# Fixed places for the first expert's weight preparation, another order at the head, and the products with v on GpSimd

## The chip, the cores and the metric

The kernel runs on one core of a Trainium2 chip. A core has a matrix engine, TensorE (PE in the profile, with its weight loads listed apart as PEld), and four more: VectorE (DVE), ScalarE (ACT), GpSimd (POOL) and SyncE (SP, which only issues DMAs here). Each engine runs its own queue strictly in order, and the queues meet through semaphores. The metric is the time of one execution on the device, in microseconds (us); a comparison is made with the median of several executions.

## The reference

Two layers follow each other. The first is a linear attention with a decaying state (B = 4 batches, H = 8 heads, S = 768 tokens, D = 48), the second a mixture of experts on its output (N = 3072 tokens of 384 features, E = 8 experts, F = 1024 hidden features, two experts a token):

```python
for t in range(S):
    cur = np.einsum('bhd,bhe->bhde', u[None] * k_t, v_t)
    y[:, :, t] = np.einsum('bhd,bhde->bhe', r_t, state + cur)
    state = w[None, :, :, None] * state + np.einsum('bhd,bhe->bhde', k_t, v_t)
x = y.transpose(0, 2, 1, 3).reshape(N, 384)

noisy = x @ w_gate + np.log1p(np.exp(x @ w_noise)) * noise
top2, top2_w = the two largest of each row, and their softmax
for e in range(E):
    for k in range(2):
        mask = top2[:, k] == e
        h = np.maximum(x[mask] @ w1[e], 0.0)
        out[mask] += top2_w[mask, k, None] * (h @ w2[e])
```

The term with `u` is the token's own: for each head it is the scalar c = sum over d of r, u and k, times the row v. This product `c * v` is called `cv` below.

## The kernel before

**Attention.** The tokens are cut into 24 tiles of 128 tokens of one batch (chunk c of 6, batch b of 4; tile i = 4c + b). For a tile, `kd` is k times powers of the decay (`prep_k`, GpSimd, two half products), `kT` and `rT` are transposes of k and r (PE `pt`, then ACT and DVE, `trans`), `pa` the scores (`scores`), `am` the scores behind the causal mask (`mask`, DVE), `py` the output from scores and state (`yout`), `pwarm` the update of the state (`kvup`), which `zup` folds into `z` and `zb`. For the token's own term GpSimd forms `rku` in four half products (`uterm_a`), DVE sums it to `c`, and `cv` is formed from `c` and `vt` in `uterm_b` (L321 to L327): in one DVE product up to tile 8, in eight ACT products, one a head, from tile 9 on. `x` = `py` + `cv` is made on DVE (`xout`) and stored to DRAM by SP; its transposes (`ptx`, `xT`) give the router's logits (`pl`, `lg`).

The program order is written out by hand: each engine's queue has the order in which the code emits. One pass of the tile loop works on several tiles at once: loads of tile i+3, `trans(i+1)`, `xtrans(i-1)`, `zup(i-1)`, `uterm_b(i+1)`, `prep_k(i+2)`, `uterm_a(i+2)`, weight steps, routing steps, `yout(i)`, `xout(i)`, `logits(i-1)`, routing steps, `scores(i+1)`, `mask(i+1)`, `kvup(i)`, routing steps.

**Routing.** After each group of 8 tiles (`GROUPS`) a long list of small DVE operations on the logits (`route`: softplus, the two largest, counts per expert) and a few matmuls into `RT` follows. It is a generator; `rstep` advances it by a given amount of credit at each point of the program where it is called, and after a step that waits for PE it skips `gap[0]` calls. `r_om` is the 0/1 matrix of chosen experts; its matmuls (L626 to L629) count the tokens ahead in each expert's list. `drop` builds the lists: from the comparisons `r_oa` and `r_ob` matmuls into `RT` (L523) put each token's number into its slot. The list of expert 0 has 7 columns of 128 slots, the lists of the other seven experts (`rest`, `drop_all`) have 49.

**Weights.** Each matmul of the experts is split for precision: a weight is a high part, `w..h` (ACT copy, L279), and the rest, `w..l` (DVE subtraction, L281), both from a staging buffer `stg` of three that one SP DMA fills. An expert has 7 units of this kind (three of w1, four of w2). A unit is a generator with stops: load, `NLAG[0]` stops, high part, stop, low part. `wstep()` moves up to three units in flight by one stop each; in the tile loop it is called twice a tile up to tile 10 and once from then on.

**Experts.** `seq` lists (expert, chunk of its token slots); expert 0 has chunks of 2, 2 and 3 tiles of slots, the last tile with 64 rows. `xgather` (GpSimd, indirect DMA) fetches rows of x, `xT` transposes them (PE `ptm`) into `xh` and `xl`, `p1` computes the hidden layer (`ph`, then `hb` on ACT and DVE, `ht` for the 64-row tile), `p2` the second matrix (`pym`, `ot`), `emit_out` scales, adds and scatters. While expert 0 runs, `rstep` and `rest_step` spread the rest of the routing over `p1` and `p2`, and `wstep` prepares expert 1's weights.

## Time and profile before

| | |
|---|---|
| median of three runs | 660.09 us (659.82 to 660.27) |
| the profiled execution | 659.12 us |
| its span, first to last instruction | 657.4 us |
| PE busy | 626.2 us (95%) |
| DVE, ACT, POOL busy | 349.4, 262.7, 262.9 us (53, 40, 40%) |
| mean granted PE clock | 0.987 |
| share of the chain that ended last: PE, DVE, ACT | 83, 11, 2% |

The span is cut into stretches below; "idle before" of an instruction is the time in which its engine had nothing to do ahead of it, with the instruction whose end released it. PE is busy nearly throughout, so what matters is where it is not, and where its clock is below full.

### The profile page before, as it was taken

What the parts mean: (1) busy time and instruction counts of PE and PEld (TensorE: products, weight loads), DVE (VectorE), ACT (ScalarE), POOL (GpSimd) and SP (SyncE); (2) the same over time, 40 slices, a digit from 0 to 9 for tenths busy, and PEclk for the clock granted to TensorE, in tenths of its full rate; (3) what the DMA queues carried; (4) which work ended last, traced back from release to release, by engine and by line L of the source; (5) the groups of instructions that cost most, each with busy time, mean ns of one, the idle gap of its engine ahead of it and who ended that gap; (6) DMA issues with size and microseconds to landing.
All of it is one profiled execution on the core that took longest, in us unless ns stands there. A gap on an engine that the chain in (4) does not pass through costs nothing.

```text
span 657.4 us, 11894 instructions
## 1 busy us (share of the span) xinstructions
PE 626.2 (95%) x4436; PEld 595.4 (91%) x4437; DVE 349.4 (53%) x883; ACT 262.7 (40%) x737; POOL 262.9 (40%) x389
## 2 busy tenths in 40 slices
PE   7999889999997889999999999999999999999993
PEld 4998789998897879999999999999999999999993
DVE  8786778797479935253452525345252534523230
ACT  1566656775323424243251524325152433523210
POOL 8775526453101247313631641363174136315211
PEclk9999979999999999999999999999999999999997
DMA  8997667773204535242533434253343425302101
GB/s 128 233 227 175 133 142 164 162 174 101 81 1 153 184 118 167 90 133 74 182 107 104 152 98 134 71 183 100 111 153 96 132 72 181 95 26 86 37 2 37
DMA packets 111444, 78.87 MB, mean 120 GB/s; under 512 B 86721, under 2 KB 101441, under 8 KB 111378
## 3 DMA queue, kind: packets, MB, share of 16 engines
q1 hardware_dynamic: 101442, 49.19, 30.2%
q0 software_dynamic: 9936, 28.83, 14.0%
q8 instruction: 37, 0.61, 0.4%
q14 instruction: 29, 0.24, 0.1%
HBM read 59.03 MB, written 19.76 MB: 120 GB/s over the span
## 4 chain that ended last, share of the span: by engine, by line
PE 83%; DVE 11%; ACT 2%; issue 2%; DMA 0%; POOL 0%; POOLq 0%; DVEq 0%; SPq 0%
PE ph L857 31%; PE pym L891 30%; PE py L396 5%; PE pa L346 3%; PE ptm L832 3%; DVE am L354 2%; PE pl L426 2%; PE py L388 2%; PE pym L884 2%; PE pt L334 2%; PE pym L882 2%; PE pwarm L364 1%; DVE RT L454 1%; PE ptx L414 1%; ACT cv L327 1%
## 5 line engine op out<-in xcount | busy, mean ns | idle before, releaser
L891 PE MATMUL pym<-w1h,hb 128*128 128x384 f32 x768 | 204.2, 339 | 0.0
L912 POOL DMA_INDIRECT out_dram<-ot,TK x56 | 57.6, 1029 | 219.9 <-DVE ot L908 200.6
L857 PE MATMUL ph<-xh,w0h 128*128 128x384 f32 (+3 forms) x408 | 142.3, 349 | 1.7 <-ACT xh L833 1.7
L891 PEld LDWEIGHTS pym<-w1h,hb 128*128 128x128 f32 x768 | 139.4, 188 | 1.1 <-issue 0.3
L857 PE MATMUL ph<-xl,w0h 128*128 128x384 f32 (+3 forms) x408 | 139.6, 342 | 0.5 <-DVE xl L834 0.2
L857 PE MATMUL ph<-xh,w0l 128*128 128x384 f32 (+3 forms) x408 | 139.4, 342 | 0.0
L861 DVE SCALAR_TENSOR_TENSOR hb<-ph,hb 128x384 fp32r<-128x384 f32 (+1 forms) x136 | 72.4, 532 | 113.9 <-ACT ht L859 68.4
L891 PE MATMUL pym<-w1l,hb 128*128 128x384 f32 x384 | 129.3, 337 | 0.0
L859 ACT ACTIVATE hb<-ph 128x384 fp32r<-128x384 f32 (+1 forms) x136 | 64.3, 473 | 120.0 <-PE ph L857 112.4
L897 ACT ACTIVATE ot<-pym 128x384 f32<-128x384 f32 x45 | 22.1, 492 | 160.4 <-PE pym L891 155.8
L805 POOL DMA_INDIRECT xg<-xd,GR x56 | 54.0, 964 | 80.1 <-DVE f L687 35.1
L857 PEld LDWEIGHTS ph<-xh,w0h 128*128 128x128 f32 x408 | 77.1, 189 | 5.1 <-ACT xh L833 2.4
L857 PEld LDWEIGHTS ph<-xl,w0h 128*128 128x128 f32 x408 | 77.1, 189 | 3.7 <-DVE xl L834 1.2
L857 PEld LDWEIGHTS ph<-xh,w0l 128*128 128x128 f32 x408 | 77.2, 189 | 2.6
L891 PEld LDWEIGHTS pym<-w1l,hb 128*128 128x128 f32 x384 | 72.2, 188 | 0.1
L834 DVE TENSOR_TENSOR xl<-ptm,xh 128x384 fp32r<-128x384 f32 (+1 forms) x56 | 28.9, 524 | 74.3 <-ACT xh L833 63.3
L814 POOL DMA_INDIRECT pv<-out_dram,GA x49 | 55.6, 1134 | 25.9 <-issue 14.9
L396 PE MATMUL py<-vt,am 128*128 128x96 f32 x384 | 60.8, 284 | 2.9 <-DVE am L354 2.0
L396 PEld LDWEIGHTS py<-vt,am 128*128 128x128 f32 x384 | 52.0, 197 | 5.1 <-DVE am L354 4.8
L307 POOL TENSOR_TENSOR kd<-kt,tabk 128x192 f32<-128x192 f32 x46 | 27.4, 617 | 57.8 <-PE pwarm L364 50.6
L281 DVE TENSOR_TENSOR w1l<-stg,w1h 128x768 fp32r<-128x768 f32 x32 | 30.8, 961 | 10.2 <-ACT w1h L279 10.2
L354 DVE TENSOR_TENSOR am<-pa,mneg 128x512 int32<-128x512 int32 x48 | 30.7, 680 | 8.8 <-PE pa L346 6.9
(205 smaller groups left out, 865.8 us busy)
## 6 DMA issues: line engine op xcount, KB each, us to landing
stg<-in_moe_w_dram SPq DMA_DIRECT2D x24, 512.0 KB, 4.2
stg<-in_moe_w_dram SPq DMA_DIRECT2D x32, 384.0 KB, 3.3
rd<-in_r_dram SPq DMA_DIRECT2D x24, 192.0 KB, 4.5
vt<-in_v_dram SPq DMA_DIRECT2D x24, 192.0 KB, 4.1
xd<-x SPq DMA_DIRECT2D x24, 192.0 KB, 2.0
out_dram<-zrow SPq DMA_DIRECT2D x16, 288.0 KB, 3.7
kt<-in_k_dram SPq DMA_DIRECT2D x23, 192.0 KB, 3.3
xg<-xd,GR POOLq DMA_INDIRECT x56
```

The costliest lines, as they stand in the source:

```text
L281: nc.vector.tensor_sub(lo, tv, hi.bitcast(F32))
L307: (eng or nc.gpsimd).tensor_mul(kd[i % 3][:, h, :D], kt[i][:, h], tabk[:, h, :D])
L354: nc.vector.tensor_tensor(am[:, s].bitcast(I32), pa[s].bitcast(I32), mneg.to_broadcast([128, NP, 128]), op=ALU.bitwise_and)
L396: nc.tensor.matmul(o2, AM[i][:, s, p, :], vt[i][:, h, None, :].to_broadcast([128, 2, D]), start=not c and h == 0, stop=h == H - 1, skip_gr ...
L805: nc.gpsimd.indirect_dma_start(out=xg[:n], out_offset=None, in_=xd[:GROUPS[GEARLY - 1][1] * 128] if early_ else xd, in_offset=bass.Indirec ...
L814: nc.gpsimd.indirect_dma_start(out=pv[:n], out_offset=None, in_=out, in_offset=bass.IndirectOffsetOnAxis(ap=GA[:n, e * NJ + t:e * NJ + t + ...
L834: nc.vector.tensor_sub(xl[:, :, o:o + n], pt[:, :, :n], xh[:, :, o:o + n].bitcast(F32))
L857: nc.tensor.matmul(ph[:, :w_], a[:, d, fs], x[:, d, :w_], start=(j == 0), stop=(j == len(q) - 1))
L859: nc.scalar.activation(h_[:, f, 0, :], ph[:, a:b], AF.Relu)
L861: nc.vector.scalar_tensor_tensor(h_[:, f, 1, :], ph[:, a:b], 0.0, h_[:, f, 0, :].bitcast(F32), op0=ALU.max, op1=ALU.subtract)
L891: nc.tensor.matmul(py, hb[:, f, a, hs], x[:, f, :], start=(j == 0), stop=(j == len(q) - 1))
L912: st = nc.gpsimd.indirect_dma_start(out=out, out_offset=bass.IndirectOffsetOnAxis(ap=TK[:n, q:q + 1], axis=0), in_=ot[:n], in_offset=None, ...
```

## The change

Four edits come together. **Weights of expert 0:** the three tables `W_LD`, `W_HI` and `W_LO` say at which tile each of the seven units is loaded, gets its high part and its low part; the calls of `wstep` in the tile loop are gone. Units 0 to 4 are finished by tile 8, the high parts of units 5 and 6 come in tiles 21 and 22, the low parts in tile 22 and behind the loop. The load and the low part stand at the end of a tile's pass, the high part where `wstep` stood. **The head:** the loads come in the order k0, r0, k1, v0, r1, u, v1; one copy of the decay's powers goes from DVE to ACT, `w128` comes later, `prep_k(1)` ahead of `uterm_a(0)`, and `prep_k(0)` with `uterm_b(0)` behind `trans(1)`. **The products `cv`** of tiles 9 to 23 are two half products on GpSimd (128 x 192 each) in place of eight on ACT. **Between attention and expert 1:** `p2(0,0)` steps the routing every 8 matmuls with a third of the credit; `gap[0]` stays 2 where it was set to 1; the credit in `p2(0,1)` is 1.2 for 1.0 and in `p1(0,2)` 1.1 for 0.75; in `p1(0,2)` expert 1's weights and next transposes get no step, in `p1(1,0)` the weights get two a step; and the transposes of expert 1's first tiles may start in `p2(0,2)` once the lists are done.

```diff
@@ -37,6 +37,10 @@
 XT_AT = 4
 LREP = 6
 NOT = 4
+
+W_LD = {1: (0,), 2: (1, 2), 4: (3,), 5: (4,), 6: (5,), 7: (6,)}
+W_HI = {4: (0,), 5: (1,), 6: (2,), 7: (3,), 8: (4,), 21: (5,), 22: (6,)}
+W_LO = {4: (0,), 5: (1,), 6: (2,), 7: (3,), 8: (4,), 22: (5,)}
 
 
 @with_exitstack
@@ -123,10 +127,12 @@
             dst[i] = t
 
     load(0, (0, 2))
+    load(1, (0, 1))
+    load(0, (2, 3))
+    load(1, (1, 2))
     ub = const.tile([128, H, D], F32, name="ub")
     nc.sync.dma_start(ub, bass.AP(tensor=u.tensor, offset=u.offset, ap=[[0, 128], [1, H * D]]))
-    load(0, (2, 3))
-    load(1)
+    load(1, (2, 3))
     load(2)
     wg = const.tile([128, ND, 2 * E], F32, name="wg")
     nc.sync.dma_start(wg[:, :, :E], w_gate.rearrange("(c p) e -> p c e", p=128))
@@ -174,9 +180,8 @@
     nc.vector.reciprocal(pwk[:, :, 64:80], tmpw[:, :, 0:16])
     nc.vector.tensor_mul(pwk[:, :, 80:96], pwk[:, :, 64:80], pwk[:, :, 79:80].to_broadcast([128, NP, 16]))
     nc.vector.tensor_mul(pwk[:, :, 96:128], pwk[:, :, 64:96], pwk[:, :, 95:96].to_broadcast([128, NP, 32]))
-    nc.vector.tensor_copy(pwr[:, :, 0:64], pwk[:, :, 127:63:-1])
+    nc.scalar.activation(pwr[:, :, 0:64], pwk[:, :, 127:63:-1], AF.Copy)
     w128 = const.tile([128, NP, 1], F32, name="w128")
-    nc.vector.tensor_mul(w128, tmpw[:, :, 63:64], tmpw[:, :, 63:64])
 
     kT, rT = {}, {}
     for src, store, pw, nm in ((kd[0], kT, pwk, "kT"), (rd[0], rT, pwr, "rT")):
@@ -193,6 +198,7 @@
     warm(WARM1)
     nc.scalar.activation(tabk.rearrange("p h d -> p (h d)"), ptab.rearrange("p a b -> p (a b)"), AF.Copy)
 
+    nc.vector.tensor_mul(w128, tmpw[:, :, 63:64], tmpw[:, :, 63:64])
     acc = const.tile([128, E], BF16, name="acc")
     spacer = const.tile([1, 1], F32, name="spacer")
     Z = [att.tile([128, NP, D], F32, name=f"z{b}", bufs=1) for b in range(B)]
@@ -258,7 +264,7 @@
 
 
     W = {}
-    NLAG = [4]
+    NLAG = [1]
 
     def w_split(e):
         W[e] = {}
@@ -323,8 +329,8 @@
         if i <= GROUPS[0][1]:
             nc.vector.tensor_mul(cv, vt[i], c8.to_broadcast([128, H, D]))
         else:
-            for h in range(H):
-                nc.scalar.activation(cv[:, h, :], vt[i][:, h, :], AF.Copy, scale=c8[:, h, :])
+            for h in (slice(0, H // 2), slice(H // 2, H)):
+                nc.gpsimd.tensor_mul(cv[:, h], vt[i][:, h], c8[:, h].to_broadcast([128, H // 2, D]))
         CV[i] = cv
 
     def trans(i):
@@ -921,16 +927,14 @@
     hold = []
 
 
-    wq.extend(w_split(0))
+    wun = w_split(0)
     consts_a()
+    prep_k(1)
     uterm_a(0)
-    prep_k(1)
     uterm_a(1)
     consts_b()
     scores(0)
     mask(0)
-    prep_k(0, nc.vector)
-    uterm_b(0)
     warm(WARM3)
     route_q = []
 
@@ -980,6 +984,9 @@
                               zrow[:96, None, :].to_broadcast([96, 2, DM]))
         if i + 1 < NT:
             trans(i + 1)
+        if i == 0:
+            prep_k(0, nc.vector)
+            uterm_b(0)
         if i:
             xtrans(i - 1)
             zup(i - 1)
@@ -992,8 +999,8 @@
         if i + 2 < NT:
             prep_k(i + 2)
             uterm_a(i + 2)
-        for _ in range(0 if i < 2 else 2 if i < 11 else 1):
-            wstep()
+        for p in W_HI.get(i, ()):
+            next(wun[p])
         rstep(STEPS_A)
         if i == 0:
             flag = consts_c()
@@ -1014,20 +1021,20 @@
             mask(i + 1)
         kvup(i)
         rstep(STEPS_KV)
+        for p in W_LO.get(i, ()) + W_LD.get(i, ()):
+            next(wun[p])
     xtrans(NT - 1)
     next(p1a)
     logits(NT - 1)
     route_when_done(NT - 1)
-    while wq or wrun:
-        wstep()
+    next(wun[6])
     NLAG[0] = 3
     for j, _ in enumerate(p1a):
         if j == XT_AT_0:
             for _ in xT(0, 1):
                 pass
         rstep(STEPS_P1)
-    for t in p2(0, 0):
-        rstep(STEPS_P2)
+    for t in p2(0, 0, lambda: rstep(STEPS_P2 / 3)):
         hold.append((0, t))
     def routes_done():
         rows(EARLY // 128, NJ)
@@ -1065,8 +1072,7 @@
             xgather(1, 0)
             tokens(NJ, E * NJ)
 
-    gap[0] = 1
-    for t in p2(0, 1, lambda: rest_step(1.0)):
+    for t in p2(0, 1, lambda: rest_step(1.2)):
         if t == 3:
             for _ in xT(0, 2):
                 pass
@@ -1086,15 +1092,18 @@
             while hold:
                 emit_out(*hold.pop(0))
             if s == 2:
-                rest_step(STEPS_P1)
-            elif XT_AT <= j < XT_AT + 2:
+                rest_step(1.1)
+                continue
+            if XT_AT <= j < XT_AT + 2:
                 next(xt, None)
             wstep()
+            if s == 3:
+                wstep()
         if s > 2 and s + 2 < len(seq):
             xgather(*seq[s + 2])
 
         for t in p2(e, ci, (lambda: rest_step(1.0)) if s == 2 else None):
-            if s > 2:
+            if s > 2 or listed[0] and t > chunks(e)[ci][0]:
                 next(xt, None)
             wstep()
             hold.append((e, t))
```

How the queues stand is seen in three places. The first is DVE in the pass of tile 10, where `r_s`, `r_sn` and `RT` are the routing list of the first group. Before:

```order
L339 TENSOR_TENSOR rT<-pt,pwr 128x512
L375 TENSOR_TENSOR zt<-pwarm,z_185 128x192
L321 TENSOR_REDUCE c_1201<-rku 128x8
L281 TENSOR_TENSOR w1l_720<-stg,w1h_719 128x768
L583 TENSOR_TENSOR r_s_1139<-RT,r_d 128x64
L584 SCALAR_TENSOR_TENSOR r_sn<-RT,nz 128x64
L586 TENSOR_SCALAR RT<-r_s_1139 128x64
L589 SCALAR_TENSOR_TENSOR RT<-RT,r_s_1139 128x64 x4
L404 TENSOR_TENSOR x<-py,cv 128x384
```

And with the change:

```order
L345 TENSOR_TENSOR rT<-pt,pwr 128x512
L381 TENSOR_TENSOR zt<-pwarm,z_185 128x192
L327 TENSOR_REDUCE c_1187<-rku 128x8
L589 TENSOR_TENSOR r_s_1125<-RT,r_d 128x64
L590 SCALAR_TENSOR_TENSOR r_sn<-RT,nz 128x64
L592 TENSOR_SCALAR RT<-r_s_1125 128x64
L595 SCALAR_TENSOR_TENSOR RT<-RT,r_s_1125 128x64 x4
L410 TENSOR_TENSOR x<-py,cv 128x384
```

The low part `w1l` no longer stands between `c` and the routing list, nor anywhere ahead of `x` in this pass; line numbers are 6 higher. The second place is GpSimd's queue in the same part of the program, where `kd` of a tile is followed by `rku` of it. Before:

```order
L307 TENSOR_TENSOR kd_83<-kt,tabk 128x4x48 x2
L314 TENSOR_TENSOR rku<-rd_87,kt 128x192 x2
L316 TENSOR_TENSOR rku<-rku,ub 128x192 x2
L307 TENSOR_TENSOR kd_84<-kt,tabk 128x4x48 x2
L314 TENSOR_TENSOR rku<-rd_88,kt 128x192 x2
L316 TENSOR_TENSOR rku<-rku,ub 128x192 x2
```

And with the change:

```order
L313 TENSOR_TENSOR kd_83<-kt,tabk 128x4x48 x2
L320 TENSOR_TENSOR rku<-rd_87,kt 128x192 x2
L322 TENSOR_TENSOR rku<-rku,ub 128x192 x2
L333 TENSOR_TENSOR cv<-vt,c_980 128x192 x2
L313 TENSOR_TENSOR kd_84<-kt,tabk 128x4x48 x2
L320 TENSOR_TENSOR rku<-rd_88,kt 128x192 x2
L322 TENSOR_TENSOR rku<-rku,ub 128x192 x2
L333 TENSOR_TENSOR cv<-vt,c_1080 128x192 x2
L313 TENSOR_TENSOR kd_85<-kt,tabk 128x4x48 x2
```

One pair `cv` a tile stands ahead of `kd` and `rku` of the tile behind it, from tile 9 on. The third place is PE between expert 0's first and second chunk: `pym` is the end of `p2(0,0)`, `ph` belongs to `p1(0,1)`. Before:

```order
L857 MATMUL ph<-xh,w0h_455 128x256
L857 MATMUL ph<-xl,w0h_455 128x256
L857 MATMUL ph<-xh,w0l_456 128x256
L626 LDWEIGHTS ltri
L626 MATMUL RT<-r_om,ltri 128x64
L628 LDWEIGHTS ones_b
L628 MATMUL RT<-r_om,ones_b 128x56
L628 LDWEIGHTS ones_b
L628 MATMUL RT<-r_om,ones_b 128x48
```

And with the change:

```order
L897 MATMUL pym<-w1l_673,hb 128x384
L897 MATMUL pym<-w1h_672,hb 128x384
L632 LDWEIGHTS ltri
L632 MATMUL RT<-r_om,ltri 128x64
L634 LDWEIGHTS ones_b
L634 MATMUL RT<-r_om,ones_b 128x56
L634 LDWEIGHTS ones_b
L634 MATMUL RT<-r_om,ones_b 128x48
```

The count matmuls of the last group (`RT<-r_om`) stood behind two of the eight hidden blocks of `p1(0,1)` and now stand ahead of the first, directly behind `pym`. In the third chunk, `p1(0,2)`, the three `w1l` that stood between the steps `r_ob` of the lists on DVE are gone; they now stand in `p1(1,0)`.

## The prediction

> **What bounds the kernel now.** I read the page's busy time and slices first, then stretches of the span, then the timeline of each engine around the stretches where TensorE is short of work.
>
> ```profile
> PE 626.2 (95%) x4436; PEld 595.4 (91%) x4437; DVE 349.4 (53%) x883; ACT 262.7 (40%) x737; POOL 262.9 (40%) x389
> ```
> ```profile
> PEclk9999979999999999999999999999999999999997
> ```
> ```profile
> 20.00:40.00 20.00, 20.00 (x248) 18.94 (x249) 15.62 (x27) 11.24 (x31) 14.05 (x25) 1.00 1.09 238
> 240.00:260.00 20.00, 17.97 (x96) 17.23 (x95) 10.98 (x18) 9.41 (x22) 13.71 (x15) 0.91 0.45 128
> 300.00:400.00 100.00, 100.00 (x567) 96.27 (x566) 43.21 (x83) 38.61 (x96) 42.88 (x52) 1.00 0.38 116
> ```
> Behind the start and length of a stretch stand the busy times of PE, PEld, DVE, ACT and POOL, then PE's granted clock. From 300 to 400 us PE is never idle, and the change edits nothing there. So the gain or loss lies in the 31.2 us (657.4 less 626.2) in which PE idles and in the two stretches at a lower clock, around 80 to 100 and 240 to 260 us. The next view cuts the attention phase at the starts of its logits matmuls (`pl`), one row a tile (i = 8 to 12):
>
> ```profile
> 55.32:61.58 6.26, 6.26 (x76) 5.99 (x74) 5.07 (x8) 4.47 (x12) 3.93 (x6) 1.00 0.58 113
> 61.58:69.34 7.76, 6.71 (x75) 6.07 (x74) 4.91 (x11) 3.80 (x12) 4.22 (x7) 1.00 0.77 190
> 69.34:77.12 7.78, 6.86 (x75) 6.13 (x75) 6.83 (x23) 5.72 (x22) 3.36 (x6) 1.00 0.85 172
> 77.12:90.09 12.97, 9.66 (x75) 8.85 (x74) 7.36 (x37) 7.37 (x26) 4.12 (x6) 0.74 0.47 106
> 90.09:96.38 6.29, 6.29 (x74) 6.02 (x74) 4.61 (x19) 3.67 (x12) 3.35 (x6) 1.00 0.78 167
> ```
> An undisturbed tile takes 6.26 us, all of it PE. Three in a row take 1.50, 1.52 and 6.71 us more.
>
> **The change part by part: weights of expert 0 and `cv`.** In tile 8 and tile 10 the same thing happens:
>
> ```profile
> 77.84 1.92 ACT L327 ACTIVATE cv<-vt,c 128x48 f32<-128x48 f32 x8
> 79.66 0.83 ACT L279 ACTIVATE w1h<-stg 128x768 fp32r<-128x768 f32 x1
> ```
> ```profile
> 62.34 1.16 PE L346 MATMUL pa<-rT,kT 64*128 64x128 f32 x16
> ```
> ```profile
> 64.25 1.06 DVE L281 TENSOR_TENSOR w1l<-stg,w1h 128x768 fp32r<-128x768 f32 x1 [2.98 <-ACT w1h L279]
> 65.24 0.55 DVE L404 TENSOR_TENSOR x<-py,cv 128x384 f32<-128x384 f32 x1
> ```
> ```profile
> 73.53 1.22 DVE L354 TENSOR_TENSOR am<-pa,mneg 128x512 int32<-128x512 int32 x2
> ```
> ```profile
> 80.53 0.96 DVE L281 TENSOR_TENSOR w1l<-stg,w1h 128x768 fp32r<-128x768 f32 x1 [4.05 <-ACT w1h L279]
> ```
> ```profile
> 83.68 0.66 PE L414 MATMUL ptx<-ident,x 128*128 128x128 f32 x2 [3.12 <-DVE RT L591]
> ```
> `w1l` heads the DVE queue and waits for `w1h`, which stands on ACT behind eight `cv` products (1.92 us). Behind `w1l` stand the routing list and `x`, and PE's transposes of `x` wait 3.12 us. The clock then falls to half (0.74 over 12.97 us is 6.7 us at half): 3.12 of waiting and some 3.4 of slow matmuls make the 6.71. In the change no weight stands in tiles 9 to 20 and no `cv` on ACT from tile 9, so tile 10 loses its chain: -6.7. In tile 8 `w1l` comes behind `am`, not ahead of `x`: -1.5. But tile 9 now carries that `w1l`. In the trace's timeline DVE runs without rest from the end of `x` (65.71) to `am` at 73.53, 7.8 us; with the 1.06 of `w1l` it is 8.9, and the tile is bound by DVE. That stretch can begin when the scores are ready, 63.5 (62.34 plus 1.16), so 2.2 us sooner; less 1.06, `am` comes 1.1 us sooner, not the 1.5 that tile 8 gains: +0.35. Bounds for the three tiles together: -8.2 (the +0.35 hidden) and -2.6 (tile 10 keeps 5.2, rival C).
>
> **`cv` on GpSimd.** The trace has no such product there. Its nearest rows are the queue's own:
>
> ```profile
> 92.45 1.16 POOL L307 TENSOR_TENSOR kd<-kt,tabk 128x192 f32<-128x192 f32 x2 [8.87 <-PE pwarm L364]
> 93.56 1.15 POOL L314 TENSOR_TENSOR rku<-rd,kt 128x192 f32<-128x192 f32 x2
> 94.67 1.14 POOL L316 TENSOR_TENSOR rku<-rku,ub 128x192 f32<-128x192 f32 x2
> 98.95 0.60 POOL L307 TENSOR_TENSOR kd<-kt,tabk 128x192 f32<-128x192 f32 x1 [3.14 <-PE pwarm L364]
> ```
> ```profile
> 94.47 0.54 DVE L321 TENSOR_REDUCE c<-rku 128x8 f32<-128x384 f32 x1
> ```
> ```profile
> 128.92 0.54 DVE L321 TENSOR_REDUCE c<-rku 128x8 f32<-128x384 f32 x1
> ```
> ```profile
> 131.83 0.44 PE L334 MATMUL pt<-ident,kd 128*128 128x128 f32 x2
> ```
> ```profile
> L316 POOL TENSOR_TENSOR rku<-rku,ub x48: 580/596/1569, 8.1 to 151.1; 128x192 f32<-128x192 f32 x48
> ```
> The new pair has their shape and two SBUF inputs: 1.15 us, bounds 2 x 0.58 and 2 x 1.57. It stands ahead of `kd` and `rku` and waits for `c` from DVE, so both now wait for DVE, which they did not. In the undisturbed tile `c` ends at 95.01, `cv` would at 96.2, `kd` at 97.3, and PE asks for it when `pwarm` is through, 98.95: 1.6 us to spare. The tightest tile: 129.46 plus 2.31 is 131.77, PE asks at 131.83. And there is a ring: `c` 0.54, `cv` 1.15, `kd` 1.16, `rku` 1.15 and 1.14, back to `c`: 5.14 us against 6.26. Both fit, so the path pays nothing for the work itself. It pays where the two engines meet:
>
> ```profile
> L324 DVE TENSOR_TENSOR cv<-vt,c x9: 558/770/916, 12.8 to 54.0; 128x384 f32<-128x384 f32 x9
> ```
> The same DVE product of two SBUF tensors takes 558 to 916 ns, up to 0.36 more beside a busy POOL. With POOL at work 4.6 of 6.26 us instead of 3.5, and now behind `c`, where the routing list runs, I take +1.0 in all; bounds 0 and +3 (eight such meetings).
>
> The Trainium skill, page SBUF — State Buffer, section "SBUF: two separate sides", speaks against this move: the port pair that VectorE and GpSimd share is an exclusive lock, and a VectorE operation with two SBUF inputs blocks until the GpSimd operation is over. By it a meeting costs up to one half product, and eight of them up to 4.8 us instead of 3; the stretch from 558 to 916 agrees in kind.
>
> **Head.** PE's waits there are:
>
> ```profile
> 8.71 0.49 PE L346 MATMUL pa<-rT,kT 64*128 64x128 f32 x4 [1.12 <-DVE rT L187]
> ```
> ```profile
> 14.46 0.79 PE L346 MATMUL pa<-rT,kT 64*128 64x128 f32 x9 [0.91 <-DVE rT L339]
> ```
> The `pwr` copy leaves DVE and `rT` of tile 1 is put ahead of `kd`, `c` and `cv` of tile 0. Both waits shrink, but `u` is loaded two places later on SP and `rku` of tile 0 stands behind `kd` of tile 1, so `c` of tile 1 comes no sooner. I take -0.5; bounds -2.0 and +0.5.
>
> SP: each weight load now stands ahead of the next tile's `kt`, `rd` and `vt`. What covers that is GpSimd, which waits for `pwarm` and hardly for data:
>
> ```profile
> POOL kd L307 <- PE pwarm L364: 50.6, 16, 8.9
> ```
> ```profile
> POOL kd L307 <- DMA kt<-in_k_dram: 1.9, 2, 1.5
> ```
> Without this cover a `kt` late by one weight load would be late on PE too; I take 0.
>
> **From attention to expert 1.** Here PE waits for the lists:
>
> ```profile
> 200.22 0.35 PE L523 MATMUL RT<-r_ob,r_oa 128*128 128x14 bf16 x8 [1.11 <-DVE r_ob L519]
> ```
> ```profile
> 207.79 0.51 PE L523 MATMUL RT<-r_ob,r_oa 128*128 128x98 bf16 x8 [1.15 <-DVE r_ob L519]
> ```
> ```profile
> 224.66 0.51 PE L523 MATMUL RT<-r_ob,r_oa 128*128 128x98 bf16 x8 [2.55 <-DVE r_ob L519]
> ```
> ```profile
> 192.03 0.43 DVE L861 SCALAR_TENSOR_TENSOR hb<-ph,hb 128x256 fp32r<-128x256 f32 x1 [2.41 <-ACT hb L859]
> ```
> ```profile
> 222.96 0.95 DVE L281 TENSOR_TENSOR w1l<-stg,w1h 128x768 fp32r<-128x768 f32 x1
> ```
> ```profile
> 241.49 0.55 PE L832 MATMUL ptm<-ident,xg 128*128 128x128 f32 x3 [1.30 <-DVE xl L834]
> 242.61 0.45 PE L857 MATMUL ph<-xh,w0h 128*128 128x384 f32 x1 [0.58 <-ACT xh L833]
> ```
> The count matmuls (`RT<-r_om`) move ahead of the second chunk's first `ph`, so DVE no longer idles 2.41 us and the list runs about 2 us earlier against PE. The 1.11 and 1.15 go; 0.3 comes back where the list reaches the three `xl`: -2.0 (0 to -2.26). Two `w1l` (0.95) leave the way to the 2.55 wait: -2.0 (0 to -2.55). One tile's `ptm` moves ahead of the 64-row tile: -1.4 of 1.30 and 0.58 (0 to -1.88). With that gap gone, so is the half clock behind it, 0.09 x 20 / 0.5 = 3.6 us long: -1.8 (0 to -1.8). The four `w1l` land in expert 1's first chunk, where DVE is busy 10.98 of 20 us; 3.8 more are covered.
>
> The Trainium skill, page TensorE: Matmul & The Clock Gate, section "HAM oscillation — how this bites in real kernels", lets the clock fall only after an idle window of 3.4 us. By it no wait here, 3.12 at most, costs clock, and this -1.8 would be 0. The trace has half clock behind 3.12 and behind 1.30 and 0.58: the trace decides.
>
> Sum: -6.7 - 1.5 + 0.35 + 1.0 - 0.5 - 2.0 - 2.0 - 1.4 - 1.8 = -14.55. The profiled execution took 659.12 us (span 657.4 and 1.7 around it) and lies 0.97 under the median of 660.09: 644.6 as profiled, **645.5 as median**. The bounds that hang together give 641 to 650 for this case.
>
> **The rivals.** A, slower: the ring of `c`, `cv`, `kd`, `rku` becomes the bound from tile 9 on. It decides from a `cv` pair of 2.25 us (5.14 + 1.1 = 6.26). With three of its eight halves at the 1.57 of the L316 row it is 5.14 + 3 x 0.97 = 8.05, 1.8 over on 14 tiles, +25: 671. For: 1.57 has occurred, and DVE's lists run in these tiles. Against: the median is 596. B: the list is bound by DVE and PE's waits only move, so the last four terms are 0: 652.7. For: DVE is full in that stretch. Against: `w1l` leaves it. C: tile 10 keeps a gap, since `kd` now waits for a `c` that the list delays, and the clock falls again; 1.5 of 6.7 is left, 650.7. For: the 131.77 against 131.83. D, it does nothing: B and C and two more us at the port, 659.9; for it speaks only that each has a ground.
>
> **How the numbers follow.** Forecast 0.56, B 0.17, C 0.12, A 0.10, D 0.05. Faster holds the forecast, B and C: 0.85; same, within 0.2% (1.3 us, about what this kernel's runs can tell), is D: 0.05; slower is A: 0.10. The range takes in the forecast, C and B with the port's upper bound, 640.5 to 656, and leaves out A, D and little else.
>
> **What would show it.** Right: tiles 8 to 12 near 6.3 us but the one with `w1l` near 8; no half clock before the tail; GpSimd pairs of `cv` near 1.2 us with `kd` done before PE asks; waits ahead of `RT<-r_ob` under 0.6 us; PE busy 97%. Wrong: PE waiting for POOL `kd` tile after tile (A), waits at `RT<-r_ob` of the old size (B), a clock of 0.5 near 80 us (C).

## The result, and the profile after

The changed kernel takes 650.86 us (median of three executions, 649.87 to 652.51) against 660.09 us before (659.82 to 660.27): a ratio of 0.9863, with a 95% interval of 0.9835 to 0.9891. The prediction was 645.5 us with a range of 640.5 to 656: the direction and the range hold, but 9.2 us were gained where 14.6 were forecast. The median also lies above the 641 to 650 us that the prediction gave for the forecast's own case. That it comes within 0.2 us of rival C's 650.7 us is a coincidence: C needs a half clock near 80 us, and there was none. The profiled execution took 650.86 us with a span of 649.1.

The page of the changed kernel, its line of busy times and its row of granted clocks:

```profile
PE 626.0 (96%) x4436; PEld 595.3 (92%) x4437; DVE 348.9 (54%) x882; ACT 236.1 (36%) x618; POOL 279.4 (43%) x419
...
PEclk9999999999998989999999999999999999999997
```

ACT lost 26.6 us of work, GpSimd took up 16.5, and PE, whose work is the same, idles 23.1 us of its span instead of 31.2. The dip of the clock near 90 us is gone; two stretches at half clock stand at a third of the span, from 204.99 and from 232.30 us, where the kernel before had one, from 243.74 us. Cut again at the starts of the logits matmuls `pl`, five rows that answer to the five shown of before; the second to the fourth are the tiles that the sum calls 8, 9 and 10 (the words "i = 8 to 12" ahead of the rows of before should have read 7 to 11):

```profile
56.35:62.61 6.26, 6.26 (x75) 5.99 (x74) 4.13 (x8) 3.98 (x12) 2.39 (x5) 1.00 0.97 205
62.61:68.87 6.26, 6.26 (x75) 5.99 (x74) 4.69 (x11) 2.52 (x6) 3.54 (x7) 1.00 1.10 244
68.87:76.69 7.82, 7.03 (x75) 6.12 (x74) 7.44 (x27) 4.04 (x14) 4.85 (x10) 1.00 0.87 181
76.69:82.95 6.26, 6.26 (x75) 5.99 (x74) 5.82 (x33) 3.28 (x10) 4.56 (x9) 1.00 0.87 187
82.95:89.21 6.26, 6.26 (x75) 5.99 (x74) 5.15 (x19) 2.96 (x10) 4.29 (x9) 1.00 0.83 194
```

7.76, 7.78 and 12.97 us have become 6.26, 7.82 and 6.26: this part came out as forecast to a few tenths. PE's waits over the whole span (us in total, times, longest) are these, the longest first:

```profile
PE ph L863 <- ACT xh L839: 2.8, 3, 1.6
PE ph L863 <- DVE hb L867: 1.9, 1, 1.9
PE ph L863 <- DVE xl L840: 1.8, 3, 1.0
PE RT L529 <- DVE r_ob L525: 1.4, 1, 1.4
```

The list's waits of the transition (1.11, 1.15 and 2.55 us at `RT<-r_ob`) are gone; the 1.4 us in the last row is in tile 21, where the kernel before waited 0.44 us. In their place PE waits for expert inputs, `xh` and `xl`, and for `hb`. Set side by side, by the starts of the same matmuls in the two profiled executions, the change of each stage is (minus is faster):

| stage | forecast | measured |
|---|---|---|
| head, to the first `pl` | -0.5 | +1.16 |
| from there to tile 8 | 0 | -0.13 |
| tile 8, tile 9, tile 10 | -1.5, +0.35, -6.7 | -1.50, +0.04, -6.71 |
| tiles 11 to 23, to the first `ph` | +1.0 | -0.35 |
| `p2(0,0)`, `p1(0,1)`, `p2(0,1)` | -2.0 | -2.74 |
| `p1(0,2)` | -2.0 | -0.33 |
| `p2(0,2)`, to expert 1's first `ph` | -1.4 | -0.57 |
| `p1(1,0)` | -1.8 | +2.58 |
| all that follows | 0 | +0.24 |
| sum | -14.55 | -8.31 |

From expert 1's second matrix on, every stage has the same length in both kernels; the +0.24 lies behind the last matmul. So 6.2 us are missing, and they are missing in two places: the head (1.7 us) and the way from `p1(0,2)` to `p1(1,0)` (6.9 us). The other stages came out 2.3 us better than forecast.

### The profile page after: what moved, and what is told of

The parts are those of the page before. It is cut to its first block, busy times and chain, and to the rows that moved or that the text cites. A ratio compares the mean times of both kernels' runs of the same rounds, so it can differ in the third digit from the quotient of the medians.

```text
span 649.1 us, 11791 instructions
## 1 busy us (share of the span) xinstructions
PE 626.0 (96%) x4436; PEld 595.3 (92%) x4437; DVE 348.9 (54%) x882; ACT 236.1 (36%) x618; POOL 279.4 (43%) x419
## 4 chain that ended last, share of the span: by engine, by line
PE 69%; DVE 3%; DMA 1%; ACT 1%; issue 0%; POOL 0%; POOLq 0%
PE ph L863 33%; PE pym L897 30%; PE ptm L838 2%; PE pym L890 2%; PE pym L888 2%; DMA stg<-in_moe_w_dram 1%; DVE xl L840 0%; DVE w1l L287 0%; DVE r_oa L516 0%; PE py L402 0%; PE RT L529 0%; DVE hb L867 0%; PE pl L432 0%; ACT hb L865 0%; DVE w0l L287 0%
## 5 line engine op out<-in xcount | busy, mean ns | idle before, releaser
L402 PE MATMUL py<-vt,am 128*128 128x96 f32 x384 | 58.9, 278 | 2.1 <-DVE am L360 1.1
L402 PEld LDWEIGHTS py<-vt,am 128*128 128x128 f32 x384 | 50.2, 192 | 4.3 <-DVE am L360 4.2
L313 POOL TENSOR_TENSOR kd<-kt,tabk 128x192 f32<-128x192 f32 x46 | 29.6, 665 | 15.3 <-DMA kt<-in_k_dram 10.0
L914 DVE SCALAR_TENSOR_TENSOR ot<-ot,GT,pv 128x384 f32<-128x384 f32 (+1 forms) x46 | 27.0, 610 | 11.0 <-ACT ot L903 10.9
```

The source lines that it names most:

```text
L313: (eng or nc.gpsimd).tensor_mul(kd[i % 3][:, h, :D], kt[i][:, h], tabk[:, h, :D])
L402: nc.tensor.matmul(o2, AM[i][:, s, p, :], vt[i][:, h, None, :].to_broadcast([128, 2, D]), start=not c and h == 0, stop=h == H - 1, skip_gr ...
L914: nc.vector.scalar_tensor_tensor(ot[:n], pt[:n], g, PV[e, t][:n], op0=ALU.mult, op1=ALU.add)
```

## The experiments

Two theories stood at the start. **Theory 1:** the attention phase gains because no `w1l` stands ahead of `x` any longer; the move of `cv` to GpSimd adds nothing. In the transition the weight steps taken out of `p1(0,2)` land where they are in the way of `xh`, `xl` and `hb`, and this eats the list's gain. **Theory 2:** the eight `cv` products that left ACT are the gain, and the transition's loss comes from elsewhere (the lists, or the clock alone). The kernels run, with the median, the spread and the ratio to the kernel before on the same chip. H4 and H2 with the new head ran on another chip than the other experiments, so where a row of theirs is set against another row the ratios are the safer measure:

| kernel | us | ratio, 95% interval |
|---|---|---|
| the change | 650.86 (649.87 to 652.51) | 0.9863, 0.9835 to 0.9891 |
| before + weight tables | 650.42 (649.47 to 651.78) | 0.9843, 0.9807 to 0.9879 |
| before + `cv` on GpSimd | 658.46 (654.14 to 659.77) | 0.9965, 0.9943 to 0.9986 |
| the change, `cv` on ACT | 650.32 (647.94 to 652.09) | 0.9823, 0.9783 to 0.9862 |
| the change, old head (H) | 648.99 (646.71 to 650.42) | 0.9807, 0.9766 to 0.9848 |
| H, one weight step (H1) | 645.33 (644.91 to 646.10) | 0.9764, 0.9747 to 0.9781 |
| H1, no weight between transposes (H2) | 644.52 (643.63 to 647.76) | 0.9768, 0.9733 to 0.9802 |
| H2, transposes of `p1(0,2)` earlier (H3) | 645.41 (643.77 to 646.42) | 0.9772, 0.9755 to 0.9790 |
| H3, `cv` on ACT | 644.41 (643.60 to 645.22) | 0.9748, 0.9731 to 0.9766 |
| H2 with the new head | 646.87 (645.39 to 648.56) | 0.9775, 0.9746 to 0.9804 |
| H2, idle matmuls (H4) | 644.06 (643.64 to 644.63) | 0.9737, 0.9710 to 0.9763 |
| H4, `cv` on ACT | 644.20 (643.60 to 646.72) | 0.9762, 0.9735 to 0.9788 |
| H4 with the new head | 646.00 (644.60 to 646.55) | 0.9782, 0.9760 to 0.9804 |

### The weight tables alone

```diff
+W_LD, W_HI, W_LO = ...          # the change's tables
-    NLAG = [4]
+    NLAG = [1]
-        for _ in range(0 if i < 2 else 2 if i < 11 else 1):
-            wstep()
+        for p in W_HI.get(i, ()):
+            next(wun[p])
...
+        for p in W_LO.get(i, ()) + W_LD.get(i, ()):
+            next(wun[p])
```

> The kernel before with the weight tables alone (cv stays on ACT, head and transition as before). Theory 1, the gain of the attention phase comes from w1l leaving the way of x: tiles 8, 9 and 10 change by about -1.5, 0 and -6.7 us, no half clock near 80 us, so about 652 us. Theory 2, it comes from the eight cv products leaving ACT: they still stand ahead of lg and kT here, PE keeps waits of about 1 us behind ACT in several tiles, and the time stays above 655 us.

650.42 us, a little under theory 1's 652 and far from theory 2's 655: one of the four edits gains as much as all four together. Tiles 8 to 10 take 6.34, 7.93 and 6.26 us, with the clock up. Of the waits behind ACT that theory 2 spoke of one is left in the tiles, 0.92 us for `lg` in tile 9.

### `cv` on GpSimd alone

```diff
-            for h in range(H):
-                nc.scalar.activation(cv[:, h, :], vt[i][:, h, :], AF.Copy, scale=c8[:, h, :])
+            for h in (slice(0, H // 2), slice(H // 2, H)):
+                nc.gpsimd.tensor_mul(cv[:, h], vt[i][:, h], c8[:, h].to_broadcast([128, H // 2, D]))
```

> The kernel before with the cv products of tiles 9 to 23 on GpSimd alone. Theory 1: w1l still stands ahead of x, but w1h no longer stands behind 1.92 us of cv, so the 3.12 us wait of tile 10 shrinks to about 1.2 us and the clock stays up: -5 to -6 us there, about 654 us. Theory 2: all of the gain is here, about 652 us, and the tiles 8 to 10 take 6.3 us each. If the port that DVE and GpSimd share costs something, tiles 11 to 23 together are over 1 us longer than before.

Half right. In the profiled execution tile 10 takes 9.41 us: `w1l` still heads DVE's queue and PE still waits for `x`, but 1.6 us instead of 3.1, and the clock stays up:

```profile
80.26 0.52 PE L414 MATMUL ptx<-ident,x 128*128 128x128 f32 x3 [1.63 <-DVE RT L591]
```

That execution, 654.14 us with a mean clock of 0.991, is the shortest of ten. The nine others took 656.95 to 659.77 at mean clocks of 0.980 to 0.989, so the median gains only 2.2 us. A single profile was not the typical one here. The mean clock differs between the executions of one kernel, which a later part of this section follows up. Tiles 11 to 23 take 83.59 us in this profile against 83.15 before, well under the 1 us named for the shared port.

### The change with `cv` on ACT, and the price of GpSimd's products

The edit is the same diff the other way round, on the changed kernel.

> The changed kernel with the cv products back on ACT. Theory 1: with no weight in tiles 9 to 20 the eight products on ACT hold nobody up, and the time is that of the changed kernel within 1 us (650 to 652). Theory 2 (the products on ACT are late for somebody): over 653 us. If GpSimd's products cost time at the port: 649 us or less.

650.32 us: no difference, as theory 1 had it. The trace of the change shows the new product (duration min/median/max in ns):

```profile
L333 POOL TENSOR_TENSOR cv<-vt,c x30: 501/507/1235, 61.9 to 160.1; 128x192 f32<-128x192 f32 x30
```

It costs 0.51 us a half, less than the 0.58 I had as the lower bound, and `kd` is done in time. What the move costs is seen in tiles 11 to 23, in one row each of the kernel before, of the change, and of the weight tables alone:

```profile
90.09:173.24 83.15, 79.72 (x888) 74.73 (x887) 63.21 (x203) 52.30 (x186) 38.94 (x64) 1.00 0.65 149
```
```profile
82.95:165.75 82.80, 79.55 (x889) 74.81 (x887) 67.33 (x204) 33.89 (x99) 56.52 (x93) 1.00 0.65 153
```
```profile
81.19:163.55 82.36, 79.70 (x888) 74.74 (x887) 63.86 (x204) 55.37 (x195) 38.84 (x64) 1.00 0.67 154
```

The weight tables gain 0.79 us there; with `cv` on GpSimd 0.44 of it is lost again. The pairs in which `cv` alone was edited agree: 82.80 us in the change against 82.35 with `cv` on ACT, and 83.59 against 83.15 in the kernel before. The loss shows at the list matmuls of tile 21, in the change and in the weight tables alone:

```profile
153.36 0.34 PE L529 MATMUL RT<-r_ob,r_oa 128*128 128x14 bf16 x8 [1.36 <-DVE r_ob L525]
```
```profile
151.15 0.34 PE L527 MATMUL RT<-r_ob,r_oa 128*128 128x14 bf16 x8 [0.44 <-DVE r_ob L523]
```

DVE's busy time in this stretch is 67.3 us instead of 63.9 for nearly the same instructions (204 in both). So with `cv` on GpSimd DVE takes 3.5 us longer for its work, and PE sees 0.44 of it.

### The old head

```diff
-    prep_k(1)
     uterm_a(0)
+    prep_k(1)
     uterm_a(1)
...
-        if i == 0:
-            prep_k(0, nc.vector)
-            uterm_b(0)
```

and with it the load order, the `pwr` copy and `w128` as before.

> The changed kernel with the head of before (load order, pwr copy on DVE, w128, prep_k and uterm_b order). The changed kernel's first logits matmul came 1.16 us later than before, with its clock granted at 10.4 us instead of 4.8 us. Theory 1: the late clock has nothing to do with the head's order; PE's waits of 1.12 and 0.91 us ahead of pa come back, and for the same clock the first pl is 1 to 2 us later than in the changed kernel: about 652 us. Theory 2: the new order is itself the loss; the first pl comes at about 19.1 us again and the time is about 649.7 us.

648.99 us, so theory 1 missed here: the old head is not slower. Theory 2's time came, but not its first `pl` at 19.1 us. It comes at 20.20 us, as late as with the new head (20.23), but for another reason: PE's clock is at half from 11.7 to 15.1 us in this execution. Of the nine other profiles with the old head, eight have the clock up there and the first `pl` at 18.3 to 19.1 us, and one, with half clock from 11.2 us on, has it at 20.0. What the new order costs is seen on GpSimd. The changed kernel:

```profile
9.21 1.14 POOL L313 TENSOR_TENSOR kd<-kt,tabk 128x192 f32<-128x192 f32 x2 [3.97 <-ACT tabk L199]
...
15.32 1.14 POOL L313 TENSOR_TENSOR kd<-kt,tabk 128x192 f32<-128x192 f32 x2
```

The same kernel with the old head:

```profile
6.07 1.15 POOL L318 TENSOR_TENSOR rku<-rd,kd 128x192 f32<-128x192 f32 x2 [0.83 <-DMA rd<-in_r_dram]
...
14.18 1.45 POOL L311 TENSOR_TENSOR kd<-kt,tabk 128x192 f32<-128x192 f32 x2
```

In the new order `kd` of tile 1 heads GpSimd's queue and waits for `tabk`; GpSimd stands still for 3.97 us that it used before for `rku` of tile 0. So `kd` of tile 2 starts 1.1 us later. In the change this is partly hidden because PE itself was slow: its clock came up at 10.4 us, where it had come at 4.8 before, so that the same 16 matmuls `pa` took 1.70 us for the first tile and 1.16 for the second:

```profile
9.28 1.70 PE L352 MATMUL pa<-rT,kT 64*128 64x128 f32 x16
...
14.08 1.16 PE L352 MATMUL pa<-rT,kT 64*128 64x128 f32 x16
```

The two waits for `rT` (1.12 and 0.91 us) on which the prediction built its gain did not come back with the old head. They stand in one of the ten profiles with this head, the one that the prediction was read from. The weight tables alone and `cv` alone leave the head as it was before, and PE waits there for `kd` of tile 1:

```profile
10.44 0.44 PE L338 MATMUL pt<-ident,kd 128*128 128x128 f32 x2 [1.27 <-POOL kd L311]
```
```profile
10.42 0.44 PE L334 MATMUL pt<-ident,kd 128*128 128x128 f32 x2 [1.41 <-POOL kd L307]
```

### One weight step in expert 1's first chunk

```diff
             wstep()
-            if s == 3:
-                wstep()
```

> The kernel of the run with the head of before (649.0 us), with one weight step instead of two after each block of p1(1,0). Theory: with two steps the pause of three steps between load and high part is half as long, ACT stands at w0h until the DMA lands (2.71 and 1.85 us) and PE waits 2.88 us for hb behind it. With one step both waits are under 0.3 us and the part from the first ph to p2(1,0) takes 2.5 to 2.9 us less at the same clock: about 646.3 us. Rival: DVE is the one that is full there with w1l and w0l; then PE's wait stays over 1.5 us and the time over 648.

645.33 us, 3.7 less than with two steps. ACT's queue in the change, in `p1(1,0)`, shows what was wrong:

```profile
241.25 1.06 ACT L285 ACTIVATE w0h<-stg 128x1024 fp32r<-128x1024 f32 x1 [1.96 <-DMA stg<-in_moe_w_dram]
243.97 1.06 ACT L285 ACTIVATE w0h<-stg 128x1024 fp32r<-128x1024 f32 x1 [1.66 <-DMA stg<-in_moe_w_dram]
244.93 0.85 ACT L865 ACTIVATE hb<-ph 128x384 fp32r<-128x384 f32 x2
```

A unit's high part comes three steps after its load. With two steps a block that is half the time, and the weights of expert 2, loaded in the same loop, had not landed when ACT reached them. ACT waited 1.96 and 1.66 us for the DMA, and two relus `hb` stood behind. PE's next matmuls had to wait until `hb` had read their PSUM buffer, 1.94 us (2.88 in the kernel with the old head, where the clock was up). With one step ACT waits for no load there:

```profile
240.40 1.06 ACT L283 ACTIVATE w0h<-stg 128x1024 fp32r<-128x1024 f32 x1
```

and PE has no wait left in the chunk behind its first two matmuls. `DVE hb` was named as releaser, but the rival, that DVE is full, falls: in the change DVE itself stood idle there and waited for ACT:

```profile
242.34 1.23 DVE L287 TENSOR_TENSOR w0l<-stg,w0h 128x1024 fp32r<-128x1024 f32 x1 [1.60 <-ACT w0h L285]
245.44 0.56 DVE L867 SCALAR_TENSOR_TENSOR hb<-ph,hb 128x384 fp32r<-128x384 f32 x1 [1.87 <-ACT hb L865]
```

The fall of the median is more than this wait. From the first `ph` to `p2(1,0)` the two profiles show 83.98 and 82.40 us, but the second has a stretch at half clock there and the first has none. The rest of the difference between these profiles is lost clock in the head of the first.

### No weight between expert 1's first transposes

```diff
-            wstep()
+            if s > 2 or t == chunks(e)[ci][0]:
+                wstep()
             hold.append((e, t))
```

> As the run with one step, and in p2(0,2) a weight step after the first tile only, so that neither w1h nor w1l stands between the three transposes of expert 1's first tiles. Theory: PE's waits there, 1.64 for xh and 0.61 for xl, are w1h (0.83 on ACT) and w1l (0.95 on DVE) ahead of the third xh and xl; they fall to about 0.8 and under 0.1: 1.3 to 1.5 us less, about 645 us. Rival: the waits are the latency of the transposes and stay over 2 us in sum; then the time stays at that of the run with one step, or rises if w1h of expert 1 is now late for p2(1,0).

In the profile PE's wait for `xh` falls from 1.64 to 0.91 us and that for `xl` from 0.61 to 0.47. So 0.73 of the first was `w1h` on ACT, which stands between the second and the third `xh` in the change:

```profile
230.21 0.83 ACT L285 ACTIVATE w1h<-stg 128x768 fp32r<-128x768 f32 x1
230.94 0.48 ACT L839 ACTIVATE xh<-ptm 128x384 fp32r<-128x384 f32 x1
```

The rest, 1.4 us, is the way of the last transposes through ACT and DVE: the expectation for `xl` was wrong (0.14 instead of over 0.5). The medians differ by 0.8 us within overlapping spreads, so the size rests on the profiles.

### Earlier transposes for `p1(0,2)`, and `cv` on ACT again

```diff
-    for t in p2(0, 1, lambda: rest_step(1.2)):
-        if t == 3:
-            for _ in xT(0, 2):
-                pass
+    def step01():
+        rest_step(1.2)
+        steps01[0] += 1
+        if steps01[0] == 4:
+            for _ in xT(0, 2):
+                pass
+    for t in p2(0, 1, step01):
```

> As the run before it, and the transposes of expert 0's third chunk stand a third into the last tile of p2(0,1), ahead of the last list steps on DVE. Theory: PE's 0.76 for xh and 1.02 for xl at the start of p1(0,2) go, with 0 to 0.5 us of new wait for the gathered rows: 1.3 to 1.8 us less, about 643.5 us. Rival: the list is what DVE is bound by there; then the wait moves to the list matmuls RT<-r_ob and less than 0.5 us is gained.

The waits of 0.76 and 1.02 us are gone as expected, and nearly as much came back: PE now waits three times for `ht` (once, 0.51 us, without the edit), whose DVE operation stands behind the list and `w0l`:

```profile
PE ph L861 <- DVE ht L865: 2.1, 3, 1.5
```

From the first `ph` to `p2(1,0)` the profiles show 80.05 us against 79.98 without the edit, and the median (645.41) shows no gain either. This is the rival in another form: DVE's queue, with the lists and three `w0l`, is the bound of that stretch, and PE's wait moves.

> As the run before it, with the cv products back on ACT. Theory: as in the pair measured above, tiles 11 to 23 take 0.4 us less and tiles 8 and 9 0.3 us more: the same time within 0.5 us, about 643.5 us.

644.41 us: the same, as expected.

### Half clock, and idle matmuls that nobody reads

Half clock appears in the profiles in stretches of 3.41 us or twice that, at different places in executions of kernels that are the same there. These are rows of windows of 3.41 us that end where the clock falls (PE's busy time is the number behind the comma; the column that says 1.00 is the clock). Kernel before:

```profile
79.90:83.31 3.41, 0.67 (x7) 0.43 (x4) 2.61 (x9) 1.14 (x3) 3.41 (x6) 1.00 0.00 0
240.32:243.74 3.42, 1.53 (x7) 1.03 (x8) 2.71 (x6) 1.39 (x6) 1.99 (x2) 1.00 0.16 58
223.26:226.67 3.41, 2.00 (x19) 2.00 (x19) 3.41 (x10) 0.08 (x1) 0.00 (x0) 1.00 0.82 226
```

The change, two windows that end at a fall and the two behind them:

```profile
201.58:204.99 3.41, 1.63 (x10) 1.27 (x11) 3.34 (x7) 2.04 (x7) 0.00 (x0) 1.00 0.27 97
228.89:232.30 3.41, 1.39 (x9) 0.86 (x7) 2.56 (x5) 2.27 (x6) 0.39 (x3) 1.00 0.16 58
```
```profile
204.99:208.40 3.41, 3.41 (x18) 3.21 (x17) 3.19 (x8) 0.61 (x3) 0.82 (x1) 0.50 0.51 142
232.30:235.71 3.41, 3.18 (x10) 3.19 (x11) 0.49 (x2) 0.22 (x1) 2.80 (x3) 0.50 0.65 196
```

The weight tables alone:

```profile
212.54:215.95 3.41, 1.00 (x13) 1.00 (x13) 3.41 (x9) 0.39 (x2) 0.00 (x0) 1.00 0.70 208
```

In each profile the changes of the clock lie whole multiples of 3.413 us apart (the change: 10.43, 204.99, 208.41, 232.30, 235.71). A fall ends a window in which PE was busy for 1.74 us or less, in 13 of the 14 falls seen (leaving the end of the kernel out). The list wait of 2.55 us is the clearest case: in the kernel before it lies across two windows (busy 2.27 and 2.00 us) and costs no clock; with the weight tables alone the same wait lies in one (busy 1.00) and costs one. Where the grid of windows lies against the kernel's start differs from execution to execution, so the same waits cost clock in one and not in another. To test this, in H2 the gaps were filled with matmuls on a tile of zeros that leave the result alone:

```diff
-WARM3 = 1
+WARM3 = 5
+    def fill(n):
+        t = psum.tile([128, 512], F32, name="pfill", tag="kv")
+        for _ in range(n):
+            nc.tensor.matmul(t, wsrc[:, :128], wsrc, start=True, stop=True)
...                                       # fill(3) behind xT(0, 2), fill(4) behind expert 1's first transposes
```

> The run with one weight step and no weights between the transposes of p2(0,2) (644.5 us; its executions lay between 643.6 and 647.8 at mean clocks of 0.995 to 0.986), with idle matmuls of 128x512 that nobody reads where PE waits: four more ahead of tile 1's kd in the head, three ahead of p1(0,2), four ahead of p1(1,0). Theory: half clock comes where PE idles for some 1.8 us or more within one of the fixed windows of 3.41 us, whose phase differs between executions; with the gaps filled there is none but the tail's, every execution shows a mean clock of 0.993 or more, and the median is about 643.5 us. Rival: the clock falls for another reason; then the executions still spread over 0.986 to 0.995 and the median stays at 644.5 or is some tenths longer.

All six executions show a mean clock of 0.993 to 0.995, and they lie between 643.64 and 644.63 us: a spread of 1.0 us where H2 had 4.1. This speaks for the theory, but H2's spread comes from one execution of four (647.76 us at 0.986). The count over all these kernels says more: of the 18 executions of H2, H3, H3 with `cv` on ACT and H2 with the new head, 7 show a mean clock under 0.993, and of the 16 of the three kernels with idle matmuls one does. With the new head it is 4 of 6 without them and none of 5 with them; with the old head it is 3 of 12 and 1 of 11, too few to tell apart. The work that PE waits for comes no earlier (79.95 us from the first `ph` to `p2(1,0)`, 79.98 in H2); what is saved is the clock. Which of the filled gaps would have cost clock is not shown, since H2's own profile lost none. The median of 644.06 us is the lowest of all kernels run, but the ratios of H2, of H3 with `cv` on ACT and of H4 overlap.

### The head, at the same clock

> The run with one weight step and no weights between the transposes of p2(0,2) (644.5 us), with the new head in place of the old one: the head alone is changed. Theory: the new head makes GpSimd wait 3 to 4 us for tabk with nothing to do, its kd of tile 2 comes 0.8 us later, and PE waits for that (2.03 and 0.42 us) in place of kd of tile 1 (1.3 and 0.2): the first pl about 1 to 1.5 us later at the same clock, so 645.5 to 646 us. Rival: the later first pl of the changed kernel was only the clock; then the first pl comes at 18.4 to 18.6 us when the clock is up, and the time is 644.5.

> The run with the idle matmuls (644.06 us), with the new head in place of the old one. Theory: 0.7 to 1.2 us longer, 644.8 to 645.3, with the first pl at about 19.2 us instead of 18.3. Rival: with the clock kept up by the idle matmuls the heads are equal within 0.3 us.

The edit is in both the new head in place of the old one, in H2 and in H4. 646.87 against 644.52, and 646.00 against 644.06 us: the new head is slower. Each of these pairs ran on two chips. On one and the same chip H4 with the new head took 646.00 and H4 with `cv` on ACT, with the old head, 644.20 us. In the profiles of the second pair no clock is lost; the first `pl` comes at 19.28 instead of 18.29 us, and from tile 9 on the difference is 0.71. PE waits for `kd` of tile 2, with the new head:

```profile
15.56 0.44 PE L346 MATMUL pt<-ident,kd 128*128 128x128 f32 x2 [1.14 <-POOL kd L319]
16.42 0.44 PE L346 MATMUL pt<-ident,kd 128*128 128x128 f32 x2 [0.43 <-POOL kd L319]
```

and with the old one for `kd` of tile 1:

```profile
10.36 0.44 PE L344 MATMUL pt<-ident,kd 128*128 128x128 f32 x2 [0.42 <-POOL kd L317]
11.03 0.44 PE L344 MATMUL pt<-ident,kd 128*128 128x128 f32 x2 [0.22 <-POOL kd L317]
```

The first `pl` came as expected, but both medians lie above what was expected, and the last two differ by more (1.9) than the profiles (0.7). What the slower executions of H4 with the new head (646.00 to 646.55 us) lose against its profiled one (644.60) stays open: the mean clock of all five is 0.995, so not every difference between executions is clock.

### `cv` on ACT, without lost clock

> The run with the idle matmuls (644.06 us, executions 643.6 to 644.6, so that a few tenths can be told now), with the cv products back on ACT. Theory: GpSimd's products cost 0.4 us in tiles 11 to 23 and save 0.3 in tiles 8 and 9, so the time is the same within 0.4 us (643.7 to 644.4); the wait ahead of the first list matmuls RT<-r_ob is 0.44 instead of 1.36 us. Rival, the move to GpSimd is a gain by itself that the throttled runs hid: 645 us or more. Rival, the shared port costs over 1 us: 643 us or less.

644.20 against 644.06 us, and in the profiles the way from the start of tile 8 to the first `ph` is 101.53 against 101.52 us. Tiles 8 and 9 take 0.5 us more and tiles 11 to 23 as much less, where 0.3 and 0.4 were expected; the wait ahead of the first `RT<-r_ob` is 0.44 instead of 1.36 us, as expected. Where `cv` stands does not matter once the weights are out of the way. One execution of five took 646.72 us at a mean clock of 0.991, so clock can still be lost.

## Why the prediction was right or wrong, step by step

- **Tiles 8 to 10 (-6.7, -1.5, +0.35): right**, in size and cause. `w1l` in front of the routing list and of `x` was the chain, and the half clock behind the 3.12 us wait went with it. What the prediction did not separate is which of the two edits does it: "no weight stands in tiles 9 to 20 and no `cv` on ACT" is two causes, of which the first gives all of it, and the second alone gave 2.2 us in the median. The +0.35 of tile 9 was hidden (+0.04).
- **`cv` on GpSimd (+1.0, bounds 0 and +3): right in kind, 0.44 measured.** `kd` was in time and the ring of rival A never bound: it needed a pair of 2.25 us, and a pair took 1.0. The table's -0.35 is this 0.44 less 0.79 that the weights' leaving gave in tiles 11 to 23, a gain that the sum had at nothing. DVE did take 3.5 us longer, but in an engine with room. The row from 558 to 916 ns was a weak ground for the price: in the kernel before, the product at 34.95 us took 558 ns although GpSimd was busy beside it throughout. By the rule of the Trainium skill, page SBUF — State Buffer, section "SBUF: two separate sides", a meeting blocks DVE for up to a whole half product; the longer DVE time agrees, and the price on the path is a small part of it.
- **Head (-0.5, bounds -2.0 and +0.5): wrong**, +0.7 to +1 at the same clock (first `pl` at 19.24 against 18.57 us in H2, 19.28 against 18.29 in H4) and +1.16 in the profile. The step that failed is "`rku` of tile 0 stands behind `kd` of tile 1, so `c` of tile 1 comes no sooner": I followed `c`, which is not what is late there, and did not follow the engine. `kd` of tile 1 waits for `tabk`, GpSimd stands still for 4 us, and `kd` of tile 2, the next thing PE asks of it, is late. The two waits on DVE that I counted are gone too, but they are also gone in all nine other profiles with the old head: they belonged to one execution, so the gain was never there to take.
- **The list's waits (-2.0, bounds 0 and -2.26): right in cause**, and with -2.74 more than the bound. The count matmuls moved and the waits of 1.11 and 1.15 us are gone, with nothing back; a wait of 0.26 us ahead of `RT<-acc` went with them, and the last 0.2 us were not traced.
- **`w1l` out of `p1(0,2)` (-2.0): the wait of 2.55 us is gone, the time is not** (-0.33). Three `xl` behind the list brought a wait of 1.02 us, and together with 0.76 for `xh` it fell into one window and cost half clock. Of rival B, "PE's waits only move", this is the part that came true. With the clock up the term is worth -1.0: `p1(0,2)` takes 13.82 us in H2 and 14.83 before.
- **`ptm` earlier (-1.4, bounds 0 to -1.88): wrong.** One `ptm` moved ahead as forecast, but `w1h` and `w1l`, no longer stepped in `p1(0,2)`, now stood between the three transposes. The gap became 1.64 + 0.61 instead of 1.30 + 0.58, so the -0.57 of the stage, inside the bounds, does not bear out the term. With the weights out of the way, in H2, the stage takes 13.59 us instead of 14.89: -1.30, as forecast.
- **The half clock behind it (-1.8): wrong**, since the gap it rests on stayed; and not only that gap decides, but how it lies against the windows.
- **"The four `w1l` land in expert 1's first chunk ... 3.8 more are covered": wrong**, and with the clock the largest miss. I counted DVE's busy time (10.98 of 20 us) and not the spacing: two steps a block also halve the time that a load has before ACT asks for it. 1.94 us on PE, 2.88 with the clock up.

Rival C (tile 10 keeps a gap) and rival D fell with tile 10; the forecast's mechanism held for the attention phase and rival B for part of the transition. H2 shows what the forecast's transition is worth when the two weight steps that failed are mended: 79.98 us from the first `ph` to `p2(1,0)` against 86.27 before, -6.3 where the last four terms made -7.2. That its median of 644.5 us then lies by the forecast's 645.5 is in part luck, since it has the old head, and tiles 11 to 23 gained what the sum had not counted. Of the prediction's own signs, "no half clock before the tail" failed twice, and waits ahead of `RT<-r_ob` under 0.6 us held but for the 1.36 in tile 21.

## What to carry to other kernels

A step that is moved off one queue's critical place is not free where it lands: follow it there with its inputs (has its load landed?), not only with its busy time. When an instruction is put first in an in-order queue, ask what it waits for and what the engine would have done meanwhile. And where the granted clock appears in a profile, judge an edit by several executions, or fill the gaps: by single profiles `cv` alone gained 5.0 us (654.14 against 659.12), by the medians 2.2.

## What the runs showed of the hardware

- Half clock came after windows of 3.41 us in which PE was busy for at most 1.74 us, about half, and not only after long waits: waits of 0.76 and 1.02 us in one window were enough, while 2.55 us across two windows were not. Not all cases fit: three windows with 1.57 (in the change, from 242.54 us), 1.73 and 1.74 us busy were followed by no fall, and H2 with the new head shows a fall after 2.05 us, at a place in tile 21 where seven other profiles have a window of 2.05 us and no fall. What counts as busy for the clock therefore stays open. The Trainium skill, page TensorE: Matmul & The Clock Gate, section "HAM oscillation — how this bites in real kernels", speaks of idle gaps of over 3.4 us; between the first and the last matmul no gap in these profiles was longer than 3.12 us, and the measurement decides.
- One such stretch cost, by estimate, 1.2 us in `p1(0,2)` of the change (14.50 us, against 14.83 before less the wait of 2.55 plus the new one of 1.02) and 1.7 in `p1(1,0)` of before (15.27 us, against 14.03 in H2 less its wait of 0.47). A slower PE may also leave the others more time: PE waited 1.94 us for `hb` 8 us behind a stretch at half clock, and 2.88 in the kernel with the old head, where the clock was up.
- The kernel before itself spread from 658.0 to 663.4 us over the executions beside these runs, at mean clocks of 0.991 to 0.979; its first three lay within 0.5 us.
